# Block 3's rows in the first part: the passes over them stand one chunk later, and VectorE takes some of them

## The chip, the cores and the metric

One core of one Trainium2 chip runs the whole kernel. The metric is the device time in microseconds of one execution; times are compared as medians over several runs. All trace times are microseconds from the start of the profiled span. Engines are named as the profile does: PE is TensorE (PEld its weight loads), DVE VectorE, ACT ScalarE, POOL GpSimd, SP SyncE, which issues the DMAs.

## What is computed

One transformer block over 2048 rows of 576 numbers: attention of 32 heads with one common key and value (18 wide), then an MLP of width 4608, both with a layer norm modulated by a condition vector. The part that matters here is the beginning, where `h` is formed and projected:

```python
x = A_x
mod = (_silu(c) @ w_mod).reshape(c.shape[0], 6, 1, -1)
sa, ca, ga, sb, cb, gb = (mod[:, 0], mod[:, 1], mod[:, 2], mod[:, 3], mod[:, 4], mod[:, 5])
h = _layernorm(x, axis=-1) * (1 + ca) + sa
x = x + ga * _A_ref(h, A_wq, A_wk, A_wv, A_wo)     # q = h @ wq, k = h @ wk, v = h @ wv, softmax(q k) v @ wo
h = _layernorm(x, axis=-1) * (1 + cb) + sb
x = x + gb * _B_ref(h, B_w1, B_b1, B_w2, B_b2)     # gelu(layernorm(h) @ w1 + b1) @ w2 + b2
```

## The kernel before

Everything is ordered by hand: each engine executes its instructions in the order in which the program text issues them, and the first to wait holds all behind it. The first part (to about 125 us) forms q, k and v; then come attention (to about 1400 us) and the MLP.

The first part goes over four blocks `tb` of 512 rows (`TB`), each in five chunks `i` of `q_chunk`. Matmuls work on split operands: a number is a rounded part (`fp32r`) and the difference to it, and a product takes three terms. For that, a block's rows `h`, transposed, stand as five slices `k` of 128 features in `zt` (traced as `big`): slice `k` rounded, slice `KD + k` the difference. `proj` makes the fourteen matmuls of a chunk (L272), slice by slice: rounded, difference, rounded again with the weights' small part. Its result in PSUM (`psB`, three buffers) is copied by ScalarE twice, as `qf` (L302) and rounded as `qs` (L303); GpSimd takes the difference (L304); SyncE stores it (L308). `qf` and `qs` have two buffers each.

Between the matmuls of a chunk `q_chunk` calls `mid`, mostly `part`: two times two matmuls of scores into a tile of `psA` (two buffers), each tile reduced to its maxima by VectorE (L368). One call comes after the seventh matmul in chunks 0 to 3 of block 2; in chunk 4 there are two calls, after the fifth and after the tenth. A third tile must wait until VectorE has reduced the first.

While block `tb` is projected, `h_chunk` prepares the slices of block `tb + 1`. For blocks 1 and 2 TensorE transposes the normalized rows. For block 3 the transposition is done by VectorE and by way of DRAM: pieces are stored to the scratch `hscr`, and `h_load(3)` (L211, L213; issued on SyncE after chunk 1 of block 2) loads them back as `Z`, five slices of rows. `h_evac` then does, for each slice:

- a pass on ScalarE that scales and shifts `Z` into `hf` (L249; `hf` has three buffers),
- a rounding, on ScalarE (L253) or, where `first` is set, on VectorE (L251),
- the difference of `hf` and the rounded slice (L254), on the engine `e`: GpSimd (`po`) or VectorE (`ve`).

For block 3 the kernel before calls `h_chunk` for slices 0 to 2 after chunk 2 of block 2 and for 3 and 4 after chunk 3, all roundings on ScalarE and all differences on GpSimd. The first chunk of block 3 follows chunk 4 of block 2 on TensorE. (The chunks are numbered here as the loop counts them, `i` = 0 to 4; what is slice `m` of the output is 4, 0, 1, 2, 3.)

Of the kernel before, what the change touches and what calls it, by code (L numbers as in the profile page):

```python
# [15 lines left out]
NB = 4  # L16
TB = S // NB
NT = TB // 128
KD = 5
# [13 lines left out]
def block_kernel(ctx: ExitStack, tc, x, wqkv, wo, w1, b1, w2, b2, c, wmod, ident_in, out):  # L33
    nc = tc.nc
    ve, ac, po, pe, sy = nc.vector, nc.scalar, nc.gpsimd, nc.tensor, nc.sync
# [17 lines left out]
    def psB(): return PS["t"].tile([128, 512], F32, name="psB", bufs=PS["b"])  # L53
# [3 lines left out]
    def big(): return per.tile([128, 10, 512], F32R, name="big", bufs=3)  # L57
# [99 lines left out]
    def tr(o, Z, k):  # L157
        pe.transpose(o, Z[:, 128 * k:128 * (k + 1)], ident)
# [18 lines left out]
    def ln1_stats(tb, t):  # L177
        X = XT[:, NT * tb + t, :]
        mv = p1.tile([128, 2], F32, name="mv1", bufs=4)
        rs = p1.tile([128, 1], F32, name="rs1", bufs=12)  # L180
        nb = p1.tile([128, 1], F32, name="nb1", bufs=12)
        ln_stats2(X, ln_stats1(X), mv, rs, nb)
        RN[tb, t] = (rs, nb)

    def ln1_apply(tb, t, e):
        if t == 0:
            Zs[tb] = p1.tile([128, NT, 640], F32, name="Z1", bufs=2)
        Z = Zs[tb]
        X = XT[:, NT * tb + t, :]
        rs, nb = RN.pop((tb, t))  # L190
        for o, i in ((Z[:, t, :D], X), (Z[:, t, D:], X[:, 512:]))[:1 if tb == NB - 1 else 2]:
            if e is ac:
                ac.activation(o, i, AF.Identity, scale=rs, bias=nb)
            else:
                ve.tensor_scalar(o, i, rs, nb, op0=ALU.mult, op1=ALU.add)
        if tb == NB - 1:
            ve.transpose(Z[:, t, :D], Z[:, t, :D])
            if t % 2:
                for p in range(0, 128, 32):
                    for i in (t - 1, t):  # L200
                        sy.dma_start(hscr[tb % 2][:, 128 * i + p:128 * i + p + 32].rearrange("(c f) n -> f c n", f=32),
                                     Z[p:p + 32, i, :D].rearrange("f (c n) -> f c n", n=32))

    def h_rows(tb):

        return Zs[tb].rearrange("p t c -> p (t c)").rearrange("p (k n) -> p k n", n=TB)

    def h_load(tb):

        H, scr = h_rows(tb), hscr[tb % 2]  # L210
        sy.dma_start(H[:, :KD - 1], scr[:512].rearrange("(k p) n -> p k n", p=128))  # L211
        for q in range(2):
            sy.dma_start(H[64 * q:64 * q + 64, KD - 1], scr[512:])  # L213
# [32 lines left out]
    def h_evac(p, zt, k, e, first=False):  # L246

        hf = p1.tile([128, TB], F32, name="hf", bufs=3)
        ac.activation(hf, p, AF.Identity, scale=mcol[:, 1, k:k + 1], bias=mcol[:, 0, k:k + 1])  # L249
        if first:  # L250
            ve.tensor_copy(zt[:, k, :], hf)  # L251
        else:
            ac.activation(zt[:, k, :], hf, AF.Copy)  # L253
        e.tensor_tensor(zt[:, KD + k, :], hf, zt[:, k, :].bitcast(F32), op=ALU.subtract)  # L254

    def h_chunk(tb, zt, k):
        if tb == NB - 1:
            p = h_rows(tb)[:, k]
        else:
            p = psB()  # L260
            for t in range(NT):
                tr(p[:, 128 * t:128 * (t + 1)], Zs[tb][:, t, :], k)
        h_evac(p, zt, k, ve if tb == 1 and k in (1, 3, 4) else po, tb == 1 and k < 3)

    def proj(o, wh, wl, c0, c1, zt, mid=None, n=0):
        terms = []
# [27 lines left out]
    def q_chunk(tb, m, zt, mid, n):  # L294

        w = 126 if m < KD - 1 else 128
        wd = 126 if m < KD - 1 else 72
        pq = psB()
        proj(pq[:w], wqh, wql, 126 * m, 126 * m + w, zt, mid, n)
        qs = p1.tile([128, 2, TB], F32R, name="qs", bufs=2)  # L300
        qf = p1.tile([128, TB], F32, name="qf", bufs=2)
        ac.activation(qf[:w], pq[:w], AF.Copy)  # L302
        ac.activation(qs[:w, 0], pq[:w], AF.Copy)  # L303
        po.tensor_tensor(qs[:w, 1], qf[:w], qs[:w, 0].bitcast(F32), op=ALU.subtract)  # L304
        if m == KD - 1:
            if tb >= 2:
                key_diff(tb, qf)
        sy.dma_start(qscr[tb, :, 126 * m:126 * m + wd, :].rearrange("s p t -> p s t"), qs[:wd].bitcast(F32))  # L308
        return qf, qs

    def k_block(tb, qs):

        pk = psB()
        for i in range(2):
            pe.matmul(pk, pick[:, i, :], qs[:, i, :], start=(i == 0), stop=(i == 1))
        ac.activation(KS[:, TB * tb:TB * (tb + 1)], pk, AF.Identity, bias=ones)

    def v_block(tb, qf):
        pk = psB()
        for i in range(NT):  # L320
            pe.transpose(pk[:, 128 * i:128 * (i + 1)], qf[:, 128 * i:128 * (i + 1)], ident)
        ve.tensor_copy(V[:, NT * tb:NT * (tb + 1), :DH],
                       pk.rearrange("p (i c) -> p i c", i=NT)[:, :, 72:72 + DH])
# [6 lines left out]
    def load_q(n):  # L330
        tb, qd = divmod(n, NQ)
        if n not in QST:
            new_q(n)
        q = QST[n]
        for g in range(2):
            for r in range(3):
                src = qscr[tb, r // 2, 4 * DH * qd:4 * DH * (qd + 1), :]
                src = src.rearrange("(p g d) t -> g d p t", p=2, g=2)[g]
                sy.dma_start(q[64 * g + DH * r:64 * g + DH * (r + 1)].bitcast(F32), src)
# [30 lines left out]
    def smax_fin1(n):  # L370
        m = MR[n] = pa.tile([128, 16], F32, name="mxf", bufs=2)
        mm = MX.pop(n)
        if n == 0:
            ve.tensor_reduce(m, mm, axis=AX.X, op=ALU.max)
        else:
            ve.tensor_reduce(m[:, :8], mm[:, :8, :], axis=AX.X, op=ALU.max)
            ve.tensor_reduce(m[:, 8:], mm[:, 8:, :3], axis=AX.X, op=ALU.max)
# [26 lines left out]
    zt = big()  # L404
# [22 lines left out]
    def dense(n, w, x):  # L427

        p = psB()
        for _ in range(n):  # L430
            pe.matmul(p, w, x, start=True, stop=True)
# [36 lines left out]
    def unit():  # L468
        nonlocal u1
        smax_half(1, u1 % 2, u1 // 2)  # L470
        u1 += 1
# [5 lines left out]
    for tb in range(NB):  # L477
        nz = big() if tb + 1 < NB else None
        for i, m in enumerate((4, 0, 1, 2, 3)):
            np_ = NPART[tb][i]  # L480
            if i == 2:
                parts.extend((u, tb) for u in range(8))
            mid = {(NB - 1, 1): unit, (NB - 1, 4): lambda: last.popleft()()}.get((tb, i), part)
            qf, qs = q_chunk(tb, m, zt, mid, np_ + 1 if np_ else 0)
            if i == 0:
                qv = qf, qs
            if i == 1:
                k_block(tb, qv[1])
                v_block(tb, qv[0])
                if tb == 0:  # L490
                    load_q(0)
            if i == 2:
                if tb == 0:
                    load_q(1)
            if tb == NB - 1:
                if i == 0:
                    unit()
                elif i == 3:
                    smax_fin1(0)
                if i == 4:  # L500
                    dense(5, wqh[:, 0, :128], KS[:, :512])
                    unit()
                    dense(4, wqh[:, 0, :128], KS[:, :512])
            if nz is not None:
                if tb == NB - 2 and i == 1:
                    h_load(tb + 1)
                for k in {1 + tb // 2: (0, 1, 2), 2 + tb // 2: (3, 4)}.get(i, ()) if tb else {3: (0, 1, 2), 4: (3, 4)}.get(i, ()):
                    h_chunk(tb + 1, nz, k)
            if tb < 2:
                for _ in range(NAPPLY[tb][i]):  # L510
                    b, t = applies.popleft()
                    ln1_apply(b, t, ve if b == 1 and t % 2 else ac)
                for _ in range(NSTAT[tb][i]):
                    ln1_stats(*stats.popleft())
        zt = nz
# [522 lines left out]
    for n in range(NQT):  # L1038
# [8 lines left out]
        for tok in order:  # L1047
            if tok[0] == "V":
                g = int(tok[1:])
                while g:  # L1050
                    i = min(g, 4 - pq % 4)
# [18 lines left out]
            elif tok == "WP":  # L1070
                h2 = part.popleft()
                p = psB()
# [495 lines left out]
```

## Time and profile before

| what | value |
|---|---|
| median of 3 runs | 2213.87 us (2212.64 to 2214.05) |
| the profiled execution | 2212.6 us, span 2210.3 us |
| TensorE busy | 2189.5 us, 99% of the span |
| VectorE busy | 1938.3 us, 88% |
| ScalarE busy | 1624.8 us, 74% |
| GpSimd busy | 1521.7 us, 69% |
| first part | about 125 us |

The span is the time between the first and the last instruction; 2.3 us of the execution lie around it. Busy time is the sum of an engine's instructions over all stages, so it doesn't say what limits one stage. Start with the chain of work that ended last, then look at where the engine that holds it is not busy, and read there, engine by engine, what each instruction waited for: the timelines give it in brackets, "idle before <- releaser".

### The profile page before, as it was taken

The page shows a single profiled execution, that of the slowest core. Times are in us where ns is not written, and L with a number is a line of the kernel's source. Part 1 is how long each engine was busy: PE and PEld are TensorE (multiplying, and loading weights), DVE is VectorE, ACT ScalarE, POOL GpSimd, SP SyncE. Part 2 cuts the span into 40 slices and gives each one's busy share as a digit, 9 for nine tenths or more (in the row PEclk, how much of TensorE's full clock was granted, in tenths as well). Part 3 has the DMA queues.
Part 4 walks back from the last instruction along what each step waited for, and adds up shares of the span by engine and source line. Part 5 has one row for each costly group of instructions (what it writes and reads, how often), then busy time and mean ns, then how long its engine had stood idle before and what let it go on. Part 6 is the DMA issues. An engine that isn't in the chain of part 4 may idle for free.

```text
span 2210.3 us, 46102 instructions
## 1 busy us (share of the span) xinstructions
PE 2189.5 (99%) x16554; PEld 1439.5 (65%) x16554; DVE 1938.3 (88%) x3425; ACT 1624.8 (74%) x3110; POOL 1521.7 (69%) x1760
## 2 busy tenths in 40 slices
PE   8999999999999999999999999999999999999999
PEld 6655444444544545444454445899898899889898
DVE  7689999999999999999999993888888878787887
ACT  5579999999999999999999998544445444343443
POOL 7654456666777678678675640888899767877776
PEclk9999999999999999999999999999999999999999
DMA  6432143433443442343343321666767746676664
GB/s 231 131 133 93 35 134 118 136 130 113 136 130 125 127 141 98 126 139 117 123 131 121 125 71 59 204 194 190 203 185 199 207 133 179 184 218 188 178 184 124
DMA packets 243688, 320.16 MB, mean 145 GB/s; under 512 B 67871, under 2 KB 133807, under 8 KB 243461
## 3 DMA queue, kind: packets, MB, share of 16 engines
q1 hardware_dynamic: 243317, 317.08, 47.0%
q8 instruction: 131, 2.15, 0.4%
q14 instruction: 96, 0.79, 0.1%
q10 hardware_dynamic: 144, 0.15, 0.0%
HBM read 207.23 MB, written 99.69 MB: 139 GB/s over the span
## 4 chain that ended last, share of the span: by engine, by line
PE 95%; DVE 2%; ACT 1%; POOL 1%; issue 1%; DMA 1%; SPq 0%; ACTq 0%; POOLq 0%; DVEq 0%
PE psC L977 24%; PE psB L1204 18%; PE psA L1307 16%; PE psB L987 14%; PE psM L343 13%; PE psB L776 2%; PE psB L997 2%; PE psA L1341 1%; PE psB L272 1%; PE psA L776 1%; PE psA L343 0%; DMA Z<-hscr 0%; DVE mx L368 0%; PE psB L381 0%; PE psM L987 0%
## 5 line engine op out<-in xcount | busy, mean ns | idle before, releaser
L989 ACT ACTIVATE P<-psB 128x512 f32<-128x512 f32 x2013 | 1054.9, 620 | 48.7 <-PE psM L343 26.9
L1009 DVE TENSOR_REDUCE mx<-psM 128x1 f32<-128x512 f32 x1476 | 931.2, 682 | 26.0 <-PE psM L343 11.0
L987 PE MATMUL psB<-qst,KS 64*128 64x512 f32 x2013 | 604.2, 433 | 0.1
L343 PE MATMUL psM<-KS,qst 64*128 64x512 f32 x1722 | 592.5, 434 | 0.4 <-DVE mx L361 0.3
L977 PE MATMUL psC<-P,V 128*32 128x256 f32 (+3 forms) x6608 | 568.1, 439 | 0.0
L987 PEld LDWEIGHTS psB<-qst,KS 64*128 64x128 f32 x2013 | 301.9, 184 | 216.2 <-ACT P L989 184.7
L343 PEld LDWEIGHTS psM<-KS,qst 64*128 64x128 f32 x1722 | 285.1, 184 | 188.4 <-DVE mx L1009 139.4
L1204 PE MATMUL psB<-ops,w1a 128*128 128x512 f32 x1512 | 393.8, 396 | 0.2 <-DVE h L1219 0.2
L1204 PEld LDWEIGHTS psB<-ops,w1a 128*128 128x128 f32 x1512 | 270.1, 188 | 46.8 <-DVE h L1219 0.6
L977 PEld LDWEIGHTS psC<-P,V 128*32 128x32 f32 x6608 | 147.0, 108 | 187.9 <-issue 160.1
L1313 DVE TENSOR_TENSOR XT<-psA,XT 128x576 f32<-128x576 f32 x330 | 241.5, 752 | 16.2 <-PE psA L1307 10.7
L1307 PEld LDWEIGHTS psA<-w2s,big 128*128 128x128 f32 x1584 | 223.7, 188 | 12.2 <-DVE XT L1313 0.2
L1307 PE MATMUL psA<-w2s,big 128*128 128x288 f32 x1584 | 230.2, 294 | 0.0
L1281 POOL TENSOR_TENSOR big<-s,big 128x512 fp32r<-128x512 f32 x132 | 171.1, 1296 | 10.6
L1007 DVE CUSTOM_DVE_ANT_0 xc<-psM,xc 128x512 f32<-128x512 f32 x246 | 165.9, 681 | 11.2 <-PE psB L987 5.7
L1217 ACT ACTIVATE psB<-gs 128x512 f32<-128x512 f32 x144 | 86.7, 602 | 120.8 <-DVE gs L1216 120.8
L1213 ACT ACTIVATE h<-psB,b1t 128x512 f32<-128x512 f32 x144 | 98.1, 681 | 105.2 <-PE psB L1204 98.7
L1000 ACT ACTIVATE xc<-psB 128x512 f32<-128x512 f32 x246 | 153.8, 625 | 3.9 <-PE psB L987 1.2
L813 POOL TENSOR_TENSOR os<-O,os 128x512 fp32r<-128x512 f32 x31 | 39.9, 1287 | 169.1 <-ACT os L812 169.1
L1216 DVE SCALAR_TENSOR_TENSOR gs<-psB,h 128x512 f32<-128x512 f32 x144 | 98.9, 687 | 38.8 <-ACT psB L1214 38.7
L847 POOL TENSOR_TENSOR r<-r,r 128x256 fp32r<-128x256 f32 (+1 forms) x162 | 122.0, 753 | 13.0
L1222 ACT ACTIVATE big<-h 128x512 fp32r<-128x512 f32 x39 | 24.7, 634 | 139.3 <-DVE h L1219 139.3
(219 smaller groups left out, 3290.4 us busy)
## 6 DMA issues: line engine op xcount, KB each, us to landing
w1a<-w1scr SPq DMA_DIRECT2D x252, 256.0 KB
w2s<-w2sum SPq DMA_DIRECT2D x132, 288.0 KB
w1scr<-r SPq DMA_DIRECT2D x126, 256.0 KB
w2s<-w2scr SPq DMA_DIRECT2D x76, 288.0 KB
w2scr<-r SPq DMA_DIRECT2D x72, 288.0 KB
w2sum<-r SPq DMA_DIRECT2D x72, 288.0 KB
qst<-qscr SPq DMA_DIRECT2D x192, 72.0 KB
w1a<-w2scr SPq DMA_DIRECT2D x33, 288.0 KB
```

What stands on the lines that cost most here:

```text
L343: pe.matmul(o, QST[n][64 * g:64 * g + 64, p, 128 * qt:128 * (qt + 1)], KS[64 * g:64 * g + 64, 512 * kb:512 * (kb + 1)], start=True, stop=True)
L847: po.tensor_tensor(o[:, n:2 * n], src, o[:, :n].bitcast(F32), op=ALU.subtract)
L977: pe.matmul(PVt[n][32 * j:32 * (j + 1), cs], V[:, kc, :], t[:, j, cs], start=(kc == 0 and h0 == 0), stop=(kc == 15), skip_group_check=True)
L987: pe.matmul(t, KS[64 * g:64 * g + 64, 128 * kc:128 * (kc + 1)], QST[n][64 * g:64 * g + 64, i, :], start=True, stop=True)
L989: ac.activation(P[n, kc][:, 2 * i + g, :], t, AF.Exp, scale=SCALE)
L1000: ac.activation(XC[-1], t, AF.Relu)
L1007: ve.tensor_tensor_reduce(c, t, c, 1.0, -3.0e38, ALU.add, ALU.max, o)
L1009: ve.tensor_reduce(o, t, axis=AX.X, op=ALU.max)
L1204: pe.matmul(o, x, y, start=(first and i == 0), stop=(i == len(terms) - 1), skip_group_check=True)
L1281: po.tensor_tensor(unit(u, 1), x, unit(u, 0).bitcast(F32), op=ALU.subtract)
L1307: pe.matmul(p[:, i, :288], x[:, ts_], W2S[k][:, y], start=(bool(first) and q == 0), stop=(q == 2), skip_group_check=True)
L1313: ve.tensor_tensor(o, p[:, :, :288], o, op=ALU.add)
```

## The change

Two lines in the first part. After it, `h_chunk` for block 3 is called for all five slices after chunk 3 of block 2 (before: slices 0 to 2 after chunk 2, slices 3 and 4 after chunk 3). And in `h_chunk`, for block 3 (`NB - 1`), the roundings of slices 0, 1 and 2 go to VectorE instead of ScalarE, and the differences of slices 1 and 3 to VectorE instead of GpSimd. Blocks 1 and 2 are prepared as before; the load from the scratch stays where it was.

```diff
@@ h_chunk
             p = psB()
             for t in range(NT):
                 tr(p[:, 128 * t:128 * (t + 1)], Zs[tb][:, t, :], k)
-        h_evac(p, zt, k, ve if tb == 1 and k in (1, 3, 4) else po, tb == 1 and k < 3)
+        on_ve = {1: (1, 3, 4), NB - 1: (1, 3)}.get(tb, ())
+        h_evac(p, zt, k, ve if k in on_ve else po, tb in (1, NB - 1) and k < 3)
@@ the loop over blocks and chunks
                 if tb == NB - 2 and i == 1:
                     h_load(tb + 1)
-                for k in {1 + tb // 2: (0, 1, 2), 2 + tb // 2: (3, 4)}.get(i, ()) if tb else {3: (0, 1, 2), 4: (3, 4)}.get(i, ()):
+                for k in ({3: (0, 1, 2), 4: (3, 4)}, {1: (0, 1, 2), 2: (3, 4)}, {3: range(KD)})[tb].get(i, ()):
                     h_chunk(tb + 1, nz, k)
```

## Rows read from the trace of the kernel before

**Rows 1.** The page, part 4: shares of the span in the chain, by engine

```profile
PE 95%; DVE 2%; ACT 1%; POOL 1%; issue 1%; DMA 1%; SPq 0%; ACTq 0%; POOLq 0%; DVEq 0%
```

**Rows 2.** Table of stretches: from:to, length, each engine's busy us (instructions), granted clock, DMA

```profile
93.20:102.22 9.02, 7.19 (x27) 3.72 (x26) 5.50 (x5) 8.00 (x14) 8.06 (x7) 1.00 0.18 61
...
125.00:2210.30 2085.30, 2080.07 (x16022) 1363.03 (x16020) 1852.01 (x3283) 1561.73 (x3001) 1446.56 (x1655) 1.00 0.47 143
```

**Rows 3.** Timeline of TensorE, 88 to 103 us: start, us, line, what, count, [idle before]

```profile
88.20 3.05 PE L272 MATMUL psB<-big,wA 128*126 128x512 f32 x12
91.18 0.73 PE L343 MATMUL psA<-KS,qst 64*128 64x512 f32 x4
...
93.19 0.50 PE L343 MATMUL psA<-KS,qst 64*128 64x512 f32 x2
94.13 0.49 PE L343 MATMUL psA<-KS,qst 64*128 64x512 f32 x2 [0.44 <-DVE mx L368]
94.55 3.13 PE L272 MATMUL psB<-big,wA 128*126 128x512 f32 x11
97.62 0.73 PE L343 MATMUL psA<-KS,qst 64*128 64x512 f32 x4
98.28 1.28 PE L272 MATMUL psB<-big,wA 128*128 128x512 f32 x3
100.56 0.96 PE L272 MATMUL psB<-big,wA 128*128 128x512 f32 x3 [0.99 <-POOL big L254]
...
102.22 0.73 PE L343 MATMUL psA<-KS,qst 64*128 64x512 f32 x4
```

**Rows 4.** Timeline of ScalarE, 92 to 97 us

```profile
92.45 0.81 ACT L249 ACTIVATE hf<-Z,mcol 128x512 f32<-128x512 f32 x1 [5.27 <-DMA Z<-hscr]
...
96.58 0.58 ACT L302 ACTIVATE qf<-psB 126x512 f32<-126x512 f32 x1
```

**Rows 5.** Timeline of VectorE, 88 to 97 us

```profile
88.08 2.36 DVE L368 TENSOR_REDUCE mx<-psA 128x2 f32<-128x1024 f32 x2 [1.76 <-PE psA L343]
91.72 4.62 DVE L368 TENSOR_REDUCE mx<-psA 128x2 f32<-128x1024 f32 x4 [1.28 <-PE psA L343]
```

**Rows 6.** Timeline of GpSimd, 94 to 102 us

```profile
94.00 4.03 POOL L254 TENSOR_TENSOR big<-hf,big 128x512 fp32r<-128x512 f32 x3 [5.47 <-ACT big L253]
...
99.24 2.50 POOL L254 TENSOR_TENSOR big<-hf,big 128x512 fp32r<-128x512 f32 x2
```

**Rows 7.** Timeline of SyncE's issues, 84 us

```profile
84.00 0.39 SPq L211 DMA_DIRECT2D Z<-hscr  x1
```

**Rows 8.** Instructions of L251 and L254 to 126 us: ns min/median/max

```profile
L251 DVE CAST big<-hf x6: 372/424/427, 19.6 to 42.3; 128x512 fp32r<-128x512 f32 x6
...
L254 POOL TENSOR_TENSOR big<-hf,big x12: 1262/1288/1301, 45.0 to 100.5; 128x512 fp32r<-128x512 f32 x12
L254 DVE TENSOR_TENSOR big<-hf,big x8: 692/693/700, 20.1 to 49.1; 128x512 fp32r<-128x512 f32 x8
```

**Rows 9.** Timelines of VectorE and of GpSimd, 24 to 29 us

```profile
25.15 1.31 DVE L415 TENSOR_TENSOR wA<-bigw,wA 128x504 fp32r<-128x504 f32 x1 [0.39 <-ACT wA L413]
26.48 1.63 DVE L419 TENSOR_TENSOR wA<-bigw,wA 64x504 fp32r<-64x504 f32 x1
...
24.22 3.36 POOL L415 TENSOR_TENSOR wA<-bigw,wA 128x504 fp32r<-128x504 f32 x2 [4.49 <-issue]
27.54 1.74 POOL L304 TENSOR_TENSOR qs<-qf,qs 128x512 fp32r<-128x512 f32 x1
```

**Rows 10.** TensorE before the clock fell; stretches, last but two number the clock; L272 alone

```profile
17.31 1.24 PE L243 MATMUL psB<-unity,modr 128*128 128x1 f32 x12 [0.43 <-DVE mcol L244]
...
18.50:19.00 0.50, 0.50 (x5) 0.50 (x4) 0.16 (x1) 0.21 (x1) 0.50 (x2) 0.79 1.08 395
...
22.00:22.50 0.50, 0.50 (x3) 0.36 (x3) 0.47 (x2) 0.47 (x2) 0.00 (x0) 0.80 1.04 387
...
21.25:22.10 0.85, 0.85 (x2) 0.75 (x3) 0.50 0.98 377
```

## Prediction

> **What bounds the kernel now.** I read the page's chain first: TensorE holds 95% of it [rows 1]. The table of stretches then says where TensorE is not busy. From 125 us to the end it idles 2085.30 - 2080.07 = 5.2 us in all, so nothing there can take up a delay; in the 9.02 us from 93.20 to 102.22 it is busy for only 7.19 [rows 2]. That stretch is the end of block 2's last chunk and block 3's first one, and the change works just ahead of it. So I read the four engines' timelines there.
>
> TensorE [rows 3]: it reaches chunk 4's second pair of maxima at 93.19, gets the second half of it at 94.13 (0.44 us waited for a VectorE reduction), then needs 94.55 to 97.62 for eleven projection matmuls and 98.28 to 102.22 for the last seven of block 3's first chunk, with 0.99 us of open waiting on a GpSimd difference. Undisturbed it makes twelve from 88.20 to 91.18, 0.248 us each. Eleven would be 2.73 (3.07 as it is) and seven 1.74 (3.94): waits cost 0.34 + 2.20 = 2.54 us here. ScalarE [rows 4] stands idle for 5.27 us up to 92.45, before the first pass over block 3's rows, because the scratch, asked for at 84.00 [rows 7], lands only then. Chunk 3's output, whose matmuls ended near 90, is copied at 96.58, behind the blocked passes. VectorE [rows 5] does chunk 4's four reductions from 91.72 to 96.34, beside all this. GpSimd [rows 6] makes three differences from 94.00 and two from 99.24, to 101.74; the last is what TensorE waits for.
>
> **The change part by part.** *Position.* Chunk 3's copies leave the queue behind the scratch and go at about 90.2 instead of 96.58. That is worth nothing by itself: chunk 3's output buffer isn't needed again until block 3's second chunk. GpSimd's difference of chunk 3 moves from behind the first three of block 3 (94.00 + 4.03 = 98.03) to about 91.2, and its store on SyncE's queue from about 99.3 to 92.5, behind the scratch's load, which SyncE had issued already. The passes themselves cannot start earlier than 92.45: nothing ahead of the load moves.
>
> *Engines.* ScalarE loses three rounding passes, GpSimd two of its five differences; both are off TensorE's path except for the 2.54 us above. VectorE gets three copies at 0.42 us and two differences at 0.69 [rows 8], 2.7 us of work. The danger is not their length but their place: they stand in VectorE's queue *ahead of* chunk 4's four reductions, and they wait for the scratch. TensorE has two psA tiles; chunk 4's second pair of maxima needs those that the first reductions free. Today VectorE starts these at 91.72; afterwards it stands on the scratch.
>
> How long it stands, step by step. First pass on ScalarE 92.45 + 0.81 = 93.26 [rows 4]. Copy 0 on VectorE, 93.31 to 93.73. Difference 0 on GpSimd, 93.80 + 1.28 = 95.08 [rows 6, 8]. Copy 1 is ready at about 94.1, when GpSimd is at work. Here I take a price from an earlier stretch: where differences on VectorE and GpSimd overlap, each waits for the other [rows 9]. VectorE's at 25.15 takes 1.31, the next 1.63, against 0.69 alone, GpSimd's at 27.54 takes 1.74 against 1.29 alone [rows 8]. The ends fit whole turns: GpSimd's pair ends at 24.22 + 3.36 = 27.58, VectorE's difference 0.53 later (28.11), GpSimd's next 1.17 after that (29.28). So copy 1 waits to 95.08 and ends near 95.4, difference 1 at 96.1, copy 2 at 96.5. GpSimd's difference 2: 96.55 to 97.83. The name hf has three buffers, so pass 3 waits until difference 0 has freed the first: 95.13 to 95.94, its rounding on ScalarE to 96.60. Difference 3 on VectorE is ready at 96.65, meets GpSimd's difference 2, and ends at 97.83 + 0.53 = 98.36. Only now come the reductions: 98.35 to 99.56, the next to 100.69 (1.13 apart, 4.62 for four [rows 5]). TensorE's second pair starts at 99.60 instead of 93.19, its second half at 100.73 instead of 94.13: 6.60 later.
>
> The Trainium skill's page "SBUF — State Buffer" (section "Who interferes with whom") says more than those rows, and speaks against this change: a VectorE instruction with two SBUF inputs, or a copy that uses both ports, and a GpSimd one that reads SBUF exclude each other for the whole instruction, whoever comes second waiting. By it the sum is the one above; the rows of 24 to 29 us agree for the differences, and no row of before shows a copy meeting GpSimd.
>
> *What comes back.* By 99.6 all rows of block 3 are ready (GpSimd's last difference ends near 99.5), so the 2.54 us of waits go. New is a wait at the end of that chunk: the two reductions inside it, 2.36 us [rows 5], start 0.54 after their matmuls (91.18 to 91.72 [rows 3, 5]) and end 2.90 after them, while TensorE wants the tile after 0.66 + 1.74 + 0.14 = 2.54: about 0.4 us. Together 6.60 - 2.54 + 0.40 = **4.5 us**.
>
> *Clock.* From 93.2 TensorE would rest for 6.4 us, run two matmuls, rest 0.6, and go on. The nearest case is early: after broken work (a wait of 0.43 before 17.31, among short matmuls) the granted clock is 0.79 in 18.50 to 19.00, then 0.50, 1.2 GHz, and 0.80 in 22.00 to 22.50, so half from about 18.8 to 22.2 [rows 10]: 3.4 us. There two projection matmuls take 0.85 us, 0.425 each against 0.248, so a us of work at half clock loses 0.42 us. I expect a fall in so long a rest. How much of the low stretch falls on work is open: 0 if the clock comes back with the first matmul, 2.1 us if 5 us of work lie in it. I take 3.4 us, the one case there is: **1.4 us**.
>
> *Sum.* 4.5 + 1.4 = 5.9 us. The profiled execution took 2212.6 us (span 2210.3 and 2.3 around it), so 2218.5 on it; it lies 1.3 below the median of the three runs, 2213.87, and to that the sum gives **2219.8**. What can't be told from no change is 0.2%, 4.4 us: above 2218.3 it is slower.
>
> **The rivals.** *B: the clock holds.* Then only 4.5: 2218.4, on the bound itself. For it: the waits of this stretch, up to 0.99 us [rows 3], leave the clock at 1.00 [rows 2]. Against: the new one is six times the longest of them.
>
> *C: VectorE and GpSimd don't hold each other here.* Then difference 1 ends by 95.3, difference 3 waits only for ScalarE's rounding (96.65 + 0.69 = 97.34), and 1.0 us goes from the sum: 4.9, 2218.8. Against it stand the four rows of [rows 9].
>
> *D: not slower.* The reductions aren't held. TensorE then loses its 2.54 us of waits and gets the 0.40: -2.1, time 2211.7. The point that decides: from landing to difference 3 the work takes 98.36 - 92.40 = 6.0 us, and a first reduction must end by 93.19, so the scratch must land by about 86.0, or VectorE take the reductions first. The landing is set by SyncE's issue at 84.00, which isn't touched, and VectorE's order is the written one; that speaks against it. The Trainium skill, "GPSIMD Engine Reference", section "4.1 Engine selection", leans this way: two-input elementwise work belongs on VectorE, GpSimd being about twice as slow. The trace agrees on the length (0.69 against 1.29 [rows 8]); by it alone the differences come sooner, and time would be D's.
>
> *E: worse.* Chunk 3's rounding writes a buffer of two, whose last store stands just ahead of the scratch's load in SyncE's queue; no row shows when it lands. If it lands with the scratch, GpSimd's difference of chunk 3 runs when copy 0 is due, and up to one such difference, 1.3 us, is added: 2221.1.
>
> **How the numbers follow.** The forecast 0.53, B 0.15, C 0.10, D 0.15, E 0.07. Predicted 2219.8. The range takes in the forecast with the clock's bounds (2218.4 to 2220.5), B, C without the clock's fall (2213.87 + 3.5 = 2217.4), E with 1 us for the spread of the runs: 2216.8 to 2222.0; D and a little of E stay out. Slower: 0.48 of the forecast, half of B (0.07), 0.05 of C, all of E (0.07), together 0.67. Within 0.2%: 0.05, 0.08, 0.05 and 0.12 of D, 0.30. Faster: 0.03 of D, for what no row shows.
>
> **What would show it.** In the timeline of after: ScalarE's first pass over the rows still at about 92.45; chunk 3's copies near 90.2; VectorE's five operations between 93.3 and 98.4, and chunk 4's first reduction after them, not at 91.7; TensorE's wait of about 6 us at 93.2, put down to that reduction; no wait on GpSimd's differences in block 3's first chunk; a granted clock of 0.50 after it; and from 125 us on the same work, some 6 us later. Wrong I would be if the reductions still start at 91.7, if the rows land earlier, or if the later stretches give something back.

## The result, and the profile after

The changed kernel takes 2219.77 us (median of 8 runs, 2218.39 to 2220.53) against 2213.21 us of the kernel before (8 runs): 6.6 us slower, ratio 1.0028 with a 95% interval of 1.0018 to 1.0039. The kernel is slower, but the interval has its low end just below the 0.2% that the prediction drew as its bound: that it is slower by more than that, to which the prediction gave 0.67, is likely and not certain. The profiled execution took 2220.53 us, the longest of the eight; its span is 2218.1. In it everything ahead of the change runs 0.73 us later than in the profile of before (a weight landed later near 11 us), so times below are compared as distances inside one trace. Lines after the change stand one lower than before: L273 is L272 of before.

The stretches answer [rows 2]; columns as there, PE, PEld, DVE, ACT, POOL, granted clock of TensorE (1.00 is full speed, 0.50 half), DMA share, GB/s.

```profile
93.20:99.70 6.50, 0.79 (x4) 0.31 (x2) 4.95 (x6) 5.00 (x7) 3.48 (x4) 0.84 0.26 91
99.70:107.40 7.70, 6.64 (x17) 4.20 (x17) 4.07 (x4) 1.08 (x2) 1.93 (x2) 0.50 0.00 0
...
131.00:2218.10 2087.10, 2081.98 (x16031) 1363.65 (x16029) 1852.26 (x3283) 1561.28 (x3001) 1444.67 (x1656) 1.00 0.47 143
```

TensorE is nearly idle for 6.5 us and then works at half clock. From 131 us on it idles 5.1 us in all, as before. From TensorE's second half of chunk 3 to its first matmul of attention (L987 of before, L988 now) it takes 128.13 - 88.20 = 39.93 us before and 136.15 - 88.93 = 47.22 now; from there to the end of the span 2082.2 and 2082.0. So all of the loss lies in these 47 us and none comes back. It is 7.3 us between these two executions and 6.6 by the medians: the profiled execution of before lies below its median, that of after above it.

TensorE's timeline, which answers [rows 3]:

```profile
88.93 3.05 PE L273 MATMUL psB<-big,wA 128*126 128x512 f32 x12
91.91 0.73 PE L344 MATMUL psA<-KS,qst 64*128 64x512 f32 x4
92.57 1.42 PE L273 MATMUL psB<-big,wA 128*126 128x512 f32 x5
100.43 0.80 PE L344 MATMUL psA<-KS,qst 64*128 64x512 f32 x2 [6.44 <-DVE mx L369]
101.56 0.80 PE L344 MATMUL psA<-KS,qst 64*128 64x512 f32 x2 [0.34 <-DVE mx L369]
102.29 5.06 PE L273 MATMUL psB<-big,wA 128*126 128x512 f32 x11
107.28 1.00 PE L344 MATMUL psA<-KS,qst 64*128 64x512 f32 x4
108.20 1.89 PE L273 MATMUL psB<-big,wA 128*128 128x512 f32 x7
110.03 1.20 PE L344 MATMUL psA<-KS,qst 64*128 64x512 f32 x4
111.16 1.20 PE L273 MATMUL psB<-big,wA 128*126 128x512 f32 x4
```

The 6.44 us before the second pair of maxima are put down to VectorE's reduction. The eleven matmuls take 4.99 us instead of 3.07 in [rows 3], though nothing interrupts them; the seven after them 1.83 instead of 3.94: the waits on GpSimd's differences are gone.

VectorE's timeline, then GpSimd's; they answer [rows 5] and [rows 6]:

```profile
94.23 0.43 DVE L251 CAST big<-hf 128x512 fp32r<-128x512 f32 x1 [3.07 <-ACT hf L249]
94.94 1.34 DVE L251 CAST big<-hf 128x512 fp32r<-128x512 f32 x1 [0.28 <-ACT hf L249]
96.32 0.69 DVE L254 TENSOR_TENSOR big<-hf,big 128x512 fp32r<-128x512 f32 x1
96.93 0.42 DVE L251 CAST big<-hf 128x512 fp32r<-128x512 f32 x1
97.55 1.69 DVE L254 TENSOR_TENSOR big<-hf,big 128x512 fp32r<-128x512 f32 x1 [0.20 <-ACT big L253]
99.16 4.61 DVE L369 TENSOR_REDUCE mx<-psA 128x2 f32<-128x1024 f32 x4
...
94.74 1.26 POOL L254 TENSOR_TENSOR big<-hf,big 128x512 fp32r<-128x512 f32 x1 [1.33 <-DVE big L251]
97.42 1.27 POOL L254 TENSOR_TENSOR big<-hf,big 128x512 fp32r<-128x512 f32 x1 [1.42 <-DVE big L251]
98.96 1.40 POOL L254 TENSOR_TENSOR big<-hf,big 128x512 fp32r<-128x512 f32 x1 [0.27 <-ACT big L253]
```

Five operations on VectorE now stand ahead of the four reductions, which began at 91.72 before. The second copy takes 1.34 us and ends 0.28 after GpSimd's difference (96.00); the second difference takes 1.69 and ends 0.55 after GpSimd's next one (98.69). The chain of waits of after runs through the hold: start, length, what.

```profile
84.73 8.57 DMA Z<-hscr
...
93.39 0.82 ACT hf L249
...
94.23 0.44 DVE big L251
...
94.74 1.27 POOL big L254
...
96.03 0.82 ACT hf L249
...
96.88 0.64 ACT big L253
...
97.55 1.69 DVE big L254
99.24 2.28 DVE mx L369 x2
```

That is the scratch's load, first pass, copy 0, GpSimd's difference 0, the pass that needed its buffer, its rounding, the delayed difference, the two reductions, and then TensorE to the end of the stretch.

### The profile page after: what moved, and what is told of

Read it like the earlier page. It is cut to its first block, busy times and chain, and to the rows that moved or that the text cites. A ratio compares the mean times of both kernels' runs of the same rounds, so it can differ in the third digit from the quotient of the medians.

```text
span 2218.1 us, 46103 instructions
## 1 busy us (share of the span) xinstructions
PE 2191.7 (99%) x16554; PEld 1441.2 (65%) x16554; DVE 1941.9 (88%) x3430; ACT 1622.7 (73%) x3107; POOL 1517.4 (68%) x1758
## 4 chain that ended last, share of the span: by engine, by line
PE 95%; DVE 2%; DMA 1%; ACT 1%; issue 0%; POOL 0%; SPq 0%; ACTq 0%; DVEq 0%; POOLq 0%
PE psC L978 24%; PE psB L1205 18%; PE psA L1308 16%; PE psB L988 14%; PE psM L344 13%; PE psB L777 2%; PE psB L273 2%; PE psB L998 2%; PE psA L1342 1%; PE psA L777 1%; PE psA L344 1%; DMA bigw<-in_wmod 0%; DMA qscr<-qs 0%; DVE mx L369 0%; DMA Z<-hscr 0%
## 5 line engine op out<-in xcount | busy, mean ns | idle before, releaser
L988 PE MATMUL psB<-qst,KS 64*128 64x512 f32 x2013 | 604.2, 433 | 0.1
L988 PEld LDWEIGHTS psB<-qst,KS 64*128 64x128 f32 x2013 | 301.8, 184 | 215.9 <-ACT P L990 184.2
```

The source lines that it names most:

```text
L988: pe.matmul(t, KS[64 * g:64 * g + 64, 128 * kc:128 * (kc + 1)], QST[n][64 * g:64 * g + 64, i, :], start=True, stop=True)
```

## The experiments

Three theories were to be told apart. **H**: the loss comes from VectorE's new operations standing ahead of chunk 4's reductions while they wait for the scratch (the *hold*); it is made longer by VectorE and GpSimd holding each other, by the three buffers, and by the clock. **P**: the later position of slices 0 to 2 does it. **L**: VectorE's added work costs its length. Medians of before in the same comparisons lay at 2213.2 to 2213.6.

### One half of the change at a time

`e1_place`, the position alone:

```diff
-        on_ve = {1: (1, 3, 4), NB - 1: (1, 3)}.get(tb, ())
-        h_evac(p, zt, k, ve if k in on_ve else po, tb in (1, NB - 1) and k < 3)
+        on_ve = {1: (1, 3, 4)}.get(tb, ())
+        h_evac(p, zt, k, ve if k in on_ve else po, tb == 1 and k < 3)
```

> Only the position is changed: all five slices of block 3 after chunk 3, every rounding on ScalarE and every difference on GpSimd as in the kernel before. Theory H (the time goes where VectorE's new operations stand ahead of chunk 4's reductions and wait for the scratch): no hold is left, so TensorE's second pair of maxima starts without a wait, and the clock stays at 1.00. GpSimd's last difference follows ScalarE's last rounding, five times 1.37 us after 92.45, so near 100.7 instead of 101.74: about 1 us faster than before, 2212.2. Rival P (moving slices 0 to 2 one chunk later does the harm, because they come late for block 3's first chunk): 2217 or more.

Measured: 2212.20 us, ratio to before 0.9993 (0.9984 to 1.0002). It is no slower, as H expected; whether the 1.4 us of gain is real the interval can't tell. P falls. TensorE's second pair starts at 93.91 without a wait; its timeline shows what is left of the waits on GpSimd:

```profile
98.74 0.97 PE L273 MATMUL psB<-big,wA 128*128 128x512 f32 x3
99.91 0.96 PE L273 MATMUL psB<-big,wA 128*128 128x512 f32 x3 [0.20 <-POOL big L254]
101.28 0.49 PE L273 MATMUL psB<-big,wA 128*128 128x512 f32 x1 [0.41 <-POOL big L254]
```

`e2_engines`, the engines alone:

```diff
-                for k in ({3: (0, 1, 2), 4: (3, 4)}, {1: (0, 1, 2), 2: (3, 4)}, {3: range(KD)})[tb].get(i, ()):
+                for k in ({3: (0, 1, 2), 4: (3, 4)}, {1: (0, 1, 2), 2: (3, 4)}, {2: (0, 1, 2), 3: (3, 4)})[tb].get(i, ()):
```

> Only the engines are changed: three roundings and two differences on VectorE, but slices 0 to 2 after chunk 2 and 3 and 4 after chunk 3, as before. Theory H: now chunk 3's two reductions are held from 88.1 to about 96.5, TensorE waits at chunk 4's first pair (91.2 to 97.7) and again a little at the second, whose reductions stand behind difference 3: no better than the whole change, 2219.5 to 2222. Rival P: with the old position the harm is gone, 2213 to 2214.

Measured: 2219.79 us, 1.0030 (1.0018 to 1.0041), as slow as the whole change, as H expected. The hold has only moved to chunk 3's reductions, and TensorE's wait to chunk 4's first pair. VectorE, then TensorE:

```profile
93.54 0.43 DVE L251 CAST big<-hf 128x512 fp32r<-128x512 f32 x1 [6.66 <-ACT hf L249]
...
96.58 2.35 DVE L369 TENSOR_REDUCE mx<-psA 128x2 f32<-128x1024 f32 x2
...
97.85 0.80 PE L344 MATMUL psA<-KS,qst 64*128 64x512 f32 x2 [6.05 <-DVE mx L369]
```

So the harm is in the choice of engines, at either position, and H's place for it is right.

### What makes the hold long

Three kernels alter the work between ScalarE's first pass and VectorE's first reduction. `e3_copies` gives VectorE the copies alone:

```diff
-        on_ve = {1: (1, 3, 4), NB - 1: (1, 3)}.get(tb, ())
+        on_ve = {1: (1, 3, 4)}.get(tb, ())
```

> The changed kernel with all five differences on GpSimd; VectorE keeps the three roundings only. Theory H: what counts is when the last of VectorE's operations ahead of the reductions ends. That is now rounding 2, about 2.2 us after the first pass ends, instead of difference 3, about 5 us after it: the reductions start some 2.6 us earlier, TensorE's wait falls from 6.4 to about 3.8 us, time 2216.5 to 2217.5. Rival L (the length of VectorE's work counts): 1.4 us of work less, 2218.4.

`e4_four` gives it two differences more (`NB - 1: (0, 1, 2, 3)`):

> The changed kernel with differences 0 to 3 on VectorE and only difference 4 on GpSimd: 1.4 us more work on VectorE. Theory H with mutual waiting of VectorE and GpSimd: rounding 1 takes 0.42 instead of 1.34 us and difference 3 0.69 instead of 1.69, since no difference runs on GpSimd beside them; the reductions start about 1.2 us earlier in spite of the added work, time about 2218.6. Rival C (they don't hold each other; 1.34 and 1.69 have another cause) and rival L (length counts): as slow as the whole change or up to 1.4 us slower, 2219.8 to 2221.2.

`e7_five` leaves the work and gives `hf` five buffers (`bufs=5`):

> The changed kernel with five buffers of hf instead of three. Theory H: pass 3 no longer waits for difference 0, its rounding ends some 0.4 us earlier, so that difference 3 on VectorE starts ahead of GpSimd's difference 2 and takes 0.69 instead of 1.69 us; the reductions start 1.2 us earlier: 2218.3 to 2218.8. Rival: the buffers are hidden behind the mutual waiting of the two engines, no change: 2219.8.

| kernel | first pass | first reduction | distance | time | ratio to before (95%) |
|---|---|---|---|---|---|
| the whole change | 93.39 | 99.16 | 5.77 | 2219.77 | 1.0028 (1.0018 to 1.0039) |
| e3_copies | 94.15 | 97.30 | 3.15 | 2216.51 | 1.0014 (1.0005 to 1.0023) |
| e4_four | 93.30 | 97.95 | 4.65 | 2218.05 | 1.0021 (1.0013 to 1.0030) |
| e7_five | 92.85 | 97.33 | 4.48 | 2218.13 | 1.0023 (1.0014 to 1.0032) |

The distances are shorter by 2.62, 1.12 and 1.29 us where 2.6, 1.2 and 1.2 were expected. With *more* work on VectorE the hold is shorter, because no difference runs on GpSimd beside it. VectorE in e4_four:

```profile
94.15 0.43 DVE L251 CAST big<-hf 128x512 fp32r<-128x512 f32 x1 [2.86 <-ACT hf L249]
94.61 0.69 DVE L254 TENSOR_TENSOR big<-hf,big 128x512 fp32r<-128x512 f32 x1
95.22 0.42 DVE L251 CAST big<-hf 128x512 fp32r<-128x512 f32 x1
...
96.74 1.29 DVE L254 TENSOR_TENSOR big<-hf,big 128x512 fp32r<-128x512 f32 x2
97.95 4.61 DVE L369 TENSOR_REDUCE mx<-psA 128x2 f32<-128x1024 f32 x4
```

Copy 1 takes 0.42 instead of 1.34 and the last difference no more than its 0.69. That last one starts at about 97.34, 4.0 us after the first pass against 4.16 in after, so of the 1.12 us nearly all is its own length. L, and the prediction's rival C, fall with this. In e7_five the rounding of slice 3 ends earlier, VectorE starts difference 3 just ahead of GpSimd's difference 2 (96.89), and again it takes 0.68:

```profile
96.73 0.68 DVE L254 TENSOR_TENSOR big<-hf,big 128x512 fp32r<-128x512 f32 x1
```

The medians fall by more than the distances: 3.3, 1.7 and 1.6 us (e7_five and e4_four come out 0.2 and 0.5 us below what was expected). What makes up the rest wasn't separated. For e3_copies and e4_four 0.3 and 0.4 us of it lie outside the profiled span. The clock can be another part: TensorE's eleven matmuls behind the hold take 4.99 us in after and e3_copies, but 4.50 in e4_four and 3.99 in e7_five. And the scratch doesn't land at the same point in each profile: the first pass starts 5.15, 4.25 and 3.90 us after chunk 3's second half, 4.46 in after.

### The place in the queue, tried the other way

`e6_behind` keeps the work on its engines and puts all but ScalarE's first three passes behind chunk 4's reductions (`h_pass` is the pass into `hf` alone, taken out of `h_evac`, which skips it where it is done):

```diff
+                if tb == NB - 2 and i == 3:
+                    for k in range(3):
+                        h_pass(h_rows(tb + 1)[:, k], k)
-                for k in ({3: (0, 1, 2), 4: (3, 4)}, {1: (0, 1, 2), 2: (3, 4)}, {3: range(KD)})[tb].get(i, ()):
+                for k in ({3: (0, 1, 2), 4: (3, 4)}, {1: (0, 1, 2), 2: (3, 4)}, {4: range(KD)})[tb].get(i, ()):
                     h_chunk(tb + 1, nz, k)
```

> The changed kernel with the same work on the same engines, but VectorE's three roundings and two differences, and all that hangs on them, stand behind chunk 4's reductions (ScalarE's first three passes stay after chunk 3). Theory H: TensorE's 6.4 us wait at the second pair is gone and the clock stays high; block 3's first chunk waits a little for the later slices (last difference near 102.5) and for VectorE's next reductions: 2214 to 2215.5. Rival L (VectorE's added work costs its length wherever it stands, or the sharing with GpSimd is the cause): 2218 or more.

Measured: 2217.30 us, 1.0019 (1.0010 to 1.0027). The expectation missed by about 2 us. The hold is gone, as H says: the second pair of maxima starts at 93.55 without a wait, its second half at 94.49 after the same 0.44 us as before. But TensorE then waits elsewhere. TensorE, and GpSimd:

```profile
94.49 0.50 PE L351 MATMUL psA<-KS,qst 64*128 64x512 f32 x2 [0.44 <-DVE mx L376]
94.91 1.19 PE L280 MATMUL psB<-big,wA 128*126 128x512 f32 x4
97.08 0.49 PE L280 MATMUL psB<-big,wA 128*128 128x512 f32 x1 [0.98 <-DVE big L258]
100.67 2.93 PE L280 MATMUL psB<-big,wA 128*128 128x512 f32 x6 [3.09 <-POOL big L261]
...
97.42 1.79 POOL L312 TENSOR_TENSOR qs<-qf,qs 126x512 fp32r<-126x512 f32 x1 [4.37 <-ACT qs L311]
99.17 4.36 POOL L261 TENSOR_TENSOR big<-hf,big 128x512 fp32r<-128x512 f32 x3
```

I had left out that chunk 4's own difference on GpSimd now stands ahead of slice 0's: 1.79 us, lengthened by VectorE's difference beside it, before the one that TensorE needs second. In the 3.09 us of rest the clock falls here too (0.57 in 99 to 100 us, then half). So H's place for the hold is borne out by the trace, but the time shows that another order alone wins little: it is the same lesson on another queue.

### What the clock costs

`e5_filler` puts 22 matmuls with unused results into TensorE's wait; `e9_full` puts 25 there and 2 between the halves of the pair:

```diff
+    fills = deque((0, 25))
+    def filled():
+        n = fills.popleft()
+        if not n:
+            part()
+            return
+        dense(n, wqh[:, 0, :128], KS[:, :512])
+        smax_part(*parts.popleft())
+        dense(2, wqh[:, 0, :128], KS[:, :512])
+        smax_part(*parts.popleft())
...
-            mid = {(NB - 1, 1): unit, (NB - 1, 4): lambda: last.popleft()()}.get((tb, i), part)
+            mid = {(NB - 1, 1): unit, (NB - 1, 4): lambda: last.popleft()(), (NB - 2, 4): filled}.get((tb, i), part)
```

(That is e9_full; e5_filler has `dense(22, ...)` and then `part()`.)

> The changed kernel with 22 matmuls of 512 columns into a spare psB tile, results unused, just ahead of chunk 4's second pair of maxima: they fill some 5.4 of the 6.4 us in which TensorE waits there and lengthen nothing. Theory K (the clock is a term of its own: half speed after the wait costs 2.5 to 3 us): the granted clock stays at 1.00, time 2216.9 to 2217.5, that is the wait alone, some 4 us above before. Rival: the loss is all in the waiting, and the matmuls after it would not run faster: 2219.8.

> As the kernel with 22 matmuls in TensorE's wait, but with 25 ahead of the second pair of maxima and 2 more between its halves, so that TensorE rests for less than half a us anywhere. Theory K: the granted clock now stays at 1.00 after the wait, and the time is the hold alone: 2216.8 to 2217.8, some 2.5 us below the whole change. Rival: the clock falls whatever stands in the wait, 2218 to 2219.

Measured: 2218.24 us for e5_filler, 1.0021 (1.0013 to 1.0030), outside what either theory expected. In the profiled execution the clock still fell for 3.5 us, after rests of only 0.95 and 0.64 us. But the eleven executions fall into two groups. The four whose mean granted clock is recorded as 1.000 take 2216.27 to 2217.47 us, near what K expected; the five at 0.998, the profiled one among them, take 2218.24 to 2219.27; the two at 0.999 take 2216.95 and 2219.28. So the filler seems to have kept the clock in some executions, and within this one kernel the groups lie 1.7 us apart (medians 2217.14 and 2218.80); in the profile the eleven matmuls take 4.31 us, 1.6 more than at full clock. e9_full takes 2217.32 us, 1.0018 (1.0009 to 1.0027), as expected, and no execution of it is below 0.999. The stretch after the filler in e5_filler, then the one around it in e9_full, then its TensorE:

```profile
101.50:105.00 3.50, 3.50 (x10) 2.78 (x9) 1.78 (x2) 1.08 (x2) 0.20 (x1) 0.51 0.00 0
```

```profile
93.00:110.00 17.00, 16.40 (x69) 10.96 (x67) 13.40 (x13) 7.21 (x11) 7.11 (x7) 1.00 0.20 68
```

```profile
101.80 2.81 PE L273 MATMUL psB<-big,wA 128*126 128x512 f32 x11
104.53 0.73 PE L344 MATMUL psA<-KS,qst 64*128 64x512 f32 x4
```

At 1.00 the eleven matmuls take 2.73 us, as the prediction had worked out from [rows 3]. So by the medians of two comparisons the clock's part is about 2219.77 - 2217.32 = 2.5 us, and the hold's, with what it gives back, 2217.32 - 2213.15 = 4.2.

### A version that beats both

The chain of after begins with the scratch's load, one DMA of 1 MB for four slices. `e8_split` takes the kernel of e1_place and loads each slice by itself; `e10_split_only` does that to the kernel before, and nothing else:

```diff
-        sy.dma_start(H[:, :KD - 1], scr[:512].rearrange("(k p) n -> p k n", p=128))
+        for k in range(KD - 1):
+            sy.dma_start(H[:, k], scr[128 * k:128 * (k + 1)])
```

> Position of the changed kernel, all roundings on ScalarE and all differences on GpSimd, and the load from the scratch in four DMAs, one for each of slices 0 to 3, instead of one. If the landing of the whole MB is what the first pass waits for, slice 0 comes some 2 us or more earlier, and the two remaining waits on GpSimd's differences in block 3's first chunk (0.20 and 0.41 us) go: 2211.4 to 2211.9. If the slices land together, 2212.2 as with the position alone.

> The kernel before with nothing changed but the load from the scratch in four DMAs, one for each of slices 0 to 3. If the earlier landing of slice 0 alone makes the gain, ScalarE's passes start near 90 instead of 92.45, GpSimd's last difference ends before TensorE asks for it, and the time is 2210.3 to 2211, as with the position moved as well. If the position is needed (chunk 3's copies behind the passes), 2211.5 to 2213.

Measured: 2210.56 us, 0.9988 (0.9979 to 0.9997), and 2210.55 us, 0.9988 (0.9979 to 0.9996): 2.6 to 2.9 us faster than before, 9.2 faster than the change. e8_split was expected 0.8 us slower than it is, e10_split_only came out as expected. With the load split, the position adds nothing that shows. ScalarE and TensorE in e10_split_only:

```profile
90.15 0.82 ACT L250 ACTIVATE hf<-Z,mcol 128x512 f32<-128x512 f32 x1 [2.04 <-DMA Z<-hscr]
...
98.89 1.89 PE L273 MATMUL psB<-big,wA 128*128 128x512 f32 x7
```

The first pass starts 2.3 us earlier than in [rows 4] (though this trace runs 0.9 us late), and the last seven matmuls of block 3's first chunk wait for nothing: 1.82 us to the next row's start instead of 3.94. By the medians 2.2 us of e10_split_only's 2.6 lie inside the span (2208.6 against 2210.8) and agree with the waits that are gone; the other 0.4 lies outside it, and no run shows why. The whole change with the load split was not run.

## Why the prediction was right, step by step

- **Where nothing changes.** The passes can't start earlier: right, 93.39 - 88.93 = 4.46 us after chunk 3's second half against 4.25 before. The prediction gave the position no worth of its own. The trace of e1_place shows some: GpSimd makes the five differences without chunk 3's between them, the last ends 12.31 us after chunk 3's second half instead of 13.54, and the eleven and the seven matmuls take 2.79 and 2.96 us instead of 3.07 and 3.94, together 1.3 less. The times can't tell this from nothing, and in the whole change the hold hides it.
- **The hold.** Forecast 5.90 us from the first pass to the first reduction (92.45 to 98.35), measured 5.77; the scratch landed 0.21 us later in after, which makes up for the difference. TensorE's second pair starts 11.50 us after 88.93 instead of 4.99 after 88.20, its second half 6.70 us later than before; forecast 6.60. Its place, ahead of chunk 4's reductions, is shown by e1_place, e2_engines and e6_behind; the mutual holding of the two engines by e4_four; the three buffers by e7_five.
- **The copy's price.** No row of before had a copy beside GpSimd; here it is 1.34 us against 0.42, and the Trainium skill's page "SBUF — State Buffer", section "Who interferes with whom", agrees with the trace in this too.
- **What comes back.** The waits are gone at full clock: eleven matmuls take 2.73 us in e9_full, seven 1.82 in e10_split_only. The prediction had taken 1.74 for the seven, so 2.46 us could come back, not 2.54. The new wait at the end of block 3's first chunk is 1.13 - 0.67 = 0.46 us; forecast 0.40. But the next pair waited before the change too, which the prediction left out:

```profile
105.40 0.73 PE L343 MATMUL psA<-KS,qst 64*128 64x512 f32 x3 [0.20 <-DVE mx L361]
```

  From 102.22 to 106.06 before is 3.84 us, from 110.03 to 114.11 after 4.08, so only 0.24 is new. Without the clock that gives 6.70 - 2.46 + 0.24 = 4.5 us, the forecast's figure, by small misses that cancel.
- **The clock, mis-sized.** Forecast 3.4 us of work at half clock and 1.4 us lost; the early case of [rows 10] was taken as its length. In the profile of after the clock is 0.82 in 97 to 98 us and 0.56 in 107 to 108, half between. TensorE worked in it from 101.56 to about 107.9, 6.3 us, and lost 0.31 in the second half of the pair, 2.26 in the eleven matmuls and 0.26 in the four after them: 2.8 us. (The seven then take 1.83, their time at full clock.) By the medians it is 2.5, still above the 2.1 that the prediction held for the most.
- **The sum.** In the two traces 4.5 + 2.8 = 7.3 us, the whole of 47.22 - 39.93. By the medians 4.5 + 1.4 = 5.9 were forecast and 4.2 + 2.5, together 6.6, measured. That 2219.77 meets 2219.8 so closely is luck: the clock's term was 1.1 us too small, the rest 0.3 too large, and the 0.7 left over was hidden in the total, since the median of before fell from 2213.87 to 2213.21 with more runs.
- **The rivals.** B: the clock did fall. C: refuted by e4_four, and by the lengths of 1.34 and 1.69 in after. D: the reductions were held; it needed a scratch that lands 6 us earlier or another order, and e6_behind shows that another order alone moves the wait to GpSimd's queue. E did not occur: GpSimd's difference of chunk 3 ended at 93.41, before copy 0 started at 94.23.

## What to carry to other kernels

An operation that waits for a transfer holds, on an engine that works in order, everything that stands behind it: ask of each moved operation what it will wait for and whose release stands behind it, on every queue it enters, before asking how fast the engine is. VectorE's 0.42 and 0.69 us against ScalarE's 0.64 and GpSimd's 1.29 were all true, and the kernel lost 6.6 us; the gain was to be had at the head of the chain, where a load in four pieces let the first one be used 2.3 us earlier.

## What the runs showed of the hardware that was not expected

After a rest of 6.4 us TensorE's granted clock stayed at half for some 6 us of matmuls that hardly paused. It isn't always so long: by the eleven matmuls' 4.50 and 3.99 us, it came back sooner in the profiles of e4_four and e7_five, after rests of 5.11 and 4.59 us; in e3_copies, after 4.51, they take 4.99 again. Stretches of after, 1 us each, columns as above:

```profile
97.00:98.00 1.00, 0.00 (x0) 0.00 (x0) 0.80 (x3) 1.00 (x2) 0.57 (x1) 0.82 0.00 0
...
102.00:103.00 1.00, 1.00 (x4) 0.62 (x3) 1.00 (x2) 0.00 (x0) 0.00 (x0) 0.50 0.00 0
...
107.00:108.00 1.00, 1.00 (x5) 0.50 (x4) 0.00 (x0) 0.00 (x0) 0.00 (x0) 0.56 0.23 82
108.00:109.00 1.00, 1.00 (x7) 0.67 (x4) 0.92 (x1) 0.00 (x0) 0.00 (x0) 1.00 0.91 295
```

And filling most of a rest was not always enough: with 22 matmuls in it, and 0.95 and 0.64 us of rest left, the clock fell all the same in the profile of e5_filler, though by their times and mean clocks not in some other executions of it; with 0.60 us of rest in all it stayed at 1.00 in the profile of e9_full. What decides wasn't tried. Nor is the early fall of [rows 10] in every execution: in the profile of e9_full the clock is 1.00 there.

```profile
18.00:23.00 5.00, 4.77 (x35) 3.77 (x33) 3.50 (x7) 3.77 (x7) 2.16 (x5) 1.00 1.06 390
```
